# Decoding 64-bit weight words with two VectorE operations and one more ScalarE operation

## The chip, the cores and the metric

The kernel runs on one core of one Trainium2 chip. The metric is the device time of one execution in microseconds; the times below are of one core and of the same program, so they are compared directly. The core has TensorE (matrix products, "PE" in the profile, its weight loads "PEld"), VectorE ("DVE"), ScalarE ("ACT"), GpSimd ("POOL") and SyncE ("SP"), which issues most of the transfers.

## The reference

The kernel computes attention with a compressive memory for 4 sequences of 576 tokens and 8 heads of 64, and feeds the result through a two-layer expert with a sigmoid gate.

```python
scores = scale * np.matmul(q, k.transpose(0, 1, 3, 2))      # causal mask, softmax -> a
local = np.matmul(a, v)
q_p = phi(q)                                                # where(q > 0, q, exp(q) - 1) + 1
mem_out = einsum(q_p, M_prev) / (einsum(q_p, z_prev)[..., None] + 1e-06)
x = g * mem_out + (1 - g) * local                           # g = sigmoid(beta), per head
h = x @ w_in                                                # 2304 x 512 by 512 x 2048
out = (h * sigmoid(1.702 * h)) @ w_out                      # by 2048 x 512
```

The two weight matrices `w_in` and `w_out` arrive as 64-bit floats, all else as 32-bit floats. The kernel reads the 64-bit numbers as pairs of 32-bit words and makes 32-bit floats of them on the chip.

## The kernel before

**Stages.** The first 256 queries of sequence 0 are handled by themselves (`first_queries`, lines 286 to 431): scores, softmax, transposes, and the memory part, for four pairs of heads. Then 16 pairs (sequence, two heads) follow in slots, with a plan that gives each step a slot and a priority (`at`, `step`, `plan_prep`, `plan_attend`). Between their steps TensorE is filled with the first expert product (`first_moe`, line 748): chunks of 256 or 320 tokens against 16 weight blocks of 128 columns, each block 12 products per chunk (4 slices of the inner dimension, times high by high, low by high and high by low parts). Its results go to DRAM (`gd`). From about 420 us on they are read back, gated, split and multiplied by the second matrix (line 988).

**Weights.** A block of weights is 128 x 512 numbers of 64 bits, a tile `wraw` of 128 x 512 x 2 whole words: index 0 of the last dimension is the lower half of a number, index 1 the upper half. Each block goes through `load` (one transfer of 512 KB on SP's queue), `scale` (ScalarE reads the upper half as a 32-bit float and multiplies it by 2^-112, which brings the exponent into the range of 32 bits), `bits` (VectorE shifts this left by 3, puts in the sign, and puts in the top three bits of the lower half), `high` (ScalarE rounds to the matrix format) and a subtraction on GpSimd for the low part. Sixteen blocks of `w_in` go this way (`conv_unit`, line 200). `w_out` has ten blocks that `decode` (line 833) handles during the attention stage and six in `conv_pair` (line 896); both use `bit_ops` (line 826). The raw tiles of `w_in` share buffers with other tiles: blocks 0, 1, 6, 7, 12 and 13 lie in a pool of two, blocks 2, 3, 10, 11, 14 and 15 in another of two, and blocks 4 and 8 as well as 5 and 9 in buffers that first hold inputs of the first queries; the load of block 4 takes the one of `fz`, which GpSimd reads at line 151 (`fqm<-fq,fz`).

**Order.** The program is recorded with a scheduler that simulates the engines and sets the order of the instructions on each. High priority, slots and manual dependences (`add_manual_dep`, without a wait where it says NOSYNC) only bound it. In `scale` such a dependence puts each decode behind the one before (`state["behind"]`). Each engine then works through its own list in that order, SP with its transfers too.

## Time and profile before

| | |
|---|---|
| runs | 616.58, 617.18, 617.86 us; median 617.18 |
| profiled execution | 620.55 us, its span 618.8 us |
| TensorE busy | 595.2 us, 96% |
| VectorE busy | 422.5 us, 68% |
| ScalarE busy | 348.0 us, 56% |
| GpSimd busy | 214.3 us, 35% |
| granted clock of TensorE | 1.0 in all slices |

The span is the time from the first to the last instruction; what lies around it makes up the rest of the execution. The page shows the span also in 40 equal slices, with the busy share of each in tenths:

```profile
PE   6799999999999999999999999999899999999997
...
DVE  5968985666668576676565435759589668856974
ACT  5667766555456445355454333356686865676451
...
DMA  8775442443255355365342114532735832471002
```

A slice is 15.5 us long. In the first two TensorE is busy 60 and 70%, later 90% or more but for two.

### The profile page before, as it was taken

Reading aid. Unit: us, or ns where it says so; the run is one execution under the profiler, and the core shown is the slowest. Engines: PE = TensorE matmul, PEld = TensorE weight load, DVE = VectorE, ACT = ScalarE, POOL = GpSimd, SP = SyncE. Lnnn points to the kernel's source line nnn. Section 1 sums busy time; section 2 is a strip of 40 time slices with the busy share of each in tenths; the row PEclk is TensorE's granted clock in tenths of the full one; section 3 lists DMA queues with packets and bytes.
Section 4 is the critical chain, followed back from the end, with each engine's and each line's share of the span. In section 5 each row is a group of like instructions: output and inputs, shape, how many; then the busy total and the mean of one; then the engine's idle time right before and its main releaser. Section 6 shows DMA issues by size and latency. Waiting matters only on the chain.

```text
span 618.8 us, 11404 instructions
## 1 busy us (share of the span) xinstructions
PE 595.2 (96%) x4000; PEld 518.2 (84%) x4000; DVE 422.5 (68%) x1022; ACT 348.0 (56%) x811; POOL 214.3 (35%) x279
## 2 busy tenths in 40 slices
PE   6799999999999999999999999999899999999997
PEld 4466767777787888887888889999799999999997
DVE  5968985666668576676565435759589668856974
ACT  5667766555456445355454333356686865676451
POOL 4756565544536235344334221141502401320000
PEclk9999999999999999999999999999999999999999
DMA  8775442443255355365342114532735832471002
GB/s 269 256 245 155 166 135 91 131 126 101 73 174 194 94 162 176 86 195 160 95 136 64 54 59 163 172 132 75 255 117 133 268 110 54 147 249 62 26 1 76
DMA packets 46985, 84.11 MB, mean 136 GB/s; under 512 B 5328, under 2 KB 33232, under 8 KB 46928
## 3 DMA queue, kind: packets, MB, share of 16 engines
q1 hardware_dynamic: 40688, 61.36, 30.4%
q0 software_dynamic: 6240, 22.02, 11.3%
q8 instruction: 31, 0.51, 0.3%
q14 instruction: 26, 0.21, 0.1%
HBM read 59.77 MB, written 23.59 MB: 135 GB/s over the span
## 4 chain that ended last, share of the span: by engine, by line
PE 70%; DVE 9%; ACT 9%; DMA 6%; issue 4%; POOL 1%; DVEq 0%; ACTq 0%; POOLq 0%; SPq 0%
PE acc L988 28%; PE pm L129 19%; PE ps L129 8%; PE po L129 7%; PE pt L138 7%; ACT a L547 2%; DMA qr<-in_vq_dram 2%; DMA gd<-hk 2%; DVE ps L541 2%; DMA wraw<-in_w_out_dram 1%; DVE qp L496 1%; DVE wo L151 1%; DVE st L151 1%; DMA g<-gd 1%; ACT wo L143 1%
## 5 line engine op out<-in xcount | busy, mean ns | idle before, releaser
L129 PE MATMUL pm<-xh,wi 128*128 128x320 f32 (+1 forms) x1024 | 218.6, 304 | 1.7 <-POOL wi L151 1.4
L129 PEld LDWEIGHTS pm<-xh,wi 128*128 128x128 f32 x1024 | 164.8, 189 | 7.4 <-issue 3.1
L988 PE MATMUL acc<-oh,wo 128*128 128x384 f32 x672 | 158.7, 337 | 2.2 <-ACT oh L143 2.2
L129 PE MATMUL pm<-xl,wi 128*128 128x256 f32 (+1 forms) x512 | 151.7, 298 | 0.1
L988 PEld LDWEIGHTS acc<-oh,wo 128*128 128x128 f32 x672 | 120.2, 188 | 3.1 <-ACT oh L143 2.9
L550 POOL TENSOR_SCALAR a<-a,sm,g 128x512 f32<-128x512 f32 (+3 forms) x112 | 76.5, 694 | 129.6 <-DVE sm L601 98.6
L151 DVE TENSOR_TENSOR ol<-g,oh 128x768 fp32r<-128x768 f32 x84 | 82.2, 981 | 46.1 <-ACT oh L143 45.8
L988 PE MATMUL acc<-ol,wo 128*128 128x384 f32 x336 | 100.5, 338 | 0.5 <-DVE ol L151 0.4
L129 PEld LDWEIGHTS pm<-xl,wi 128*128 128x128 f32 x512 | 96.4, 189 | 0.5 <-DVE xl L151 0.3
L547 ACT ACTIVATE a<-ps,nm 128x256 f32<-128x256 f32 (+2 forms) x112 | 59.8, 540 | 65.6 <-DVE nm L541 65.6
L143 ACT ACTIVATE oh<-g 128x768 fp32r<-128x768 f32 x84 | 70.4, 842 | 44.0 <-PE acc L988 32.7
L541 DVE CUSTOM_DVE_ANT_0 ps<-ps,mask 128x256 f32<-128x256 f32 (+4 forms) x144 | 67.2, 506 | 38.8 <-PE ps L129 37.9
L129 PE MATMUL ps<-kqf 128*128 128x288 f32 (+4 forms) x288 | 71.4, 478 | 3.0 <-ACT at L547 1.4
L935 POOL DMA_DIRECT2D g<-gd x48 | 34.7, 724 | 114.3 <-DVE ol L151 66.3
L988 PEld LDWEIGHTS acc<-ol,wo 128*128 128x128 f32 x336 | 61.9, 188 | 1.8 <-DVE ol L151 1.7
L143 ACT ACTIVATE hk<-pm 128x256 f32<-128x256 f32 (+1 forms) x76 | 30.8, 408 | 44.3 <-PE pm L129 36.9
L138 PE MATMUL pt<-ident,a 128*128 128x128 f32 x296 | 53.2, 273 | 0.1
L941 ACT ACTIVATE g<-g 128x768 f32<-128x768 f32 x48 | 39.7, 839 | 15.9 <-DMA g<-gd 13.5
L129 PEld LDWEIGHTS po<-e,vr 128*64 128x64 f32 x416 | 29.9, 137 | 20.1
L151 DVE TENSOR_TENSOR g<-g,g 128x768 f32<-128x768 f32 x48 | 45.6, 951 | 0.0
L129 PE MATMUL po<-e,vr 128*64 128x320 f32 (+3 forms) x416 | 45.4, 359 | 0.0
L129 PEld LDWEIGHTS ps<-kqf 64*128 64x128 f32 (+1 forms) x288 | 30.3, 189 | 15.1 <-issue 5.3
(126 smaller groups left out, 776.6 us busy)
## 6 DMA issues: line engine op xcount, KB each, us to landing
g<-gd POOLq DMA_DIRECT2D x48, 384.0 KB, 4.7
gd<-hk SPq DMA_DIRECT2D x64, 160.0 KB, 1.9
wraw<-in_w_in_dram SPq DMA_DIRECT2D x16, 512.0 KB, 5.1
gd<-hk SPq DMA_DIRECT2D x64, 128.0 KB, 2.0
kqf<-in_kq_dram SPq DMA_DIRECT2D x12, 608.0 KB, 5.6
vr<-in_vq_dram SPq DMA_DIRECT2D x16, 320.0 KB, 4.9
wraw<-in_w_out_dram SPq DMA_DIRECT2D x10, 512.0 KB, 4.0
qr<-in_vq_dram SPq DMA_DIRECT2D x12, 320.0 KB, 3.0
```

The costliest lines, as they stand in the source:

```text
L129: x = nc.tensor.matmul(out, l, r, start=start, stop=stop)
L138: state["att"] = nc.tensor.transpose(out, in_, idn).ins.name
L143: return nc.scalar.activation(out=dst, in_=src, func=AF.Copy, **kw)
L151: return (nc.vector if eng == "V" else nc.gpsimd).tensor_tensor(out=dst, in0=a, in1=b, op=op)
L496: nc.vector.scalar_tensor_tensor(out=P["qp"][:, T0:].rearrange("p t (h d) -> p t h d", h=2), in0=qv(), scalar=0.0, in1=qm, op0=ALU.max, op ...
L541: nc.vector.tensor_tensor_reduce(out=ps, in0=ps, in1=mk, op0=ALU.add, op1=ALU.min, scale=-0.125, scalar=1e38 if j == 0 else nm[:, j - 1:j] ...
L547: return nc.scalar.activation(out=a, in_=ps, func=AF.Exp, scale=-1.0, bias=nm, accum_out=sm)
L550: return (nc.vector if eng == "V" else nc.gpsimd).tensor_scalar(out=a, in0=a, scalar1=r, scalar2=gcol, op0=ALU.mult, op1=ALU.mult)
L935: x = nc.gpsimd.dma_start(t, gd[4 * kh + p][:, :, t0:t0 + QN].rearrange("i p t -> p i t"))
L941: x = nc.scalar.activation(out=t, in_=t, func=AF.Gelu_apprx_sigmoid)
L988: nc.tensor.matmul(acc[b, j][:, :QN], W[2 * p + kk][:, WPART[i], sp, 128 * j:128 * j + 128], mv[:, kk], start=first and p + kk == 0 and sp ...
```

## The change

A new helper `low_words` is one ScalarE instruction per block: it reads the lower halves as unsigned whole numbers, multiplies by 0.936 x 2^-29, and writes the nearest whole number (0 to 7) back to the place of the lower half. `bit_ops` moves up and is now used by all three places. It shifts the scaled upper half left by 3 and puts in that number in one VectorE instruction, and puts in the sign in a second one; the shift as an instruction of its own is gone. In `conv_unit` and `conv_pair` the result goes straight to the second tile. In `conv_unit` the next block's scaling is put behind `low_words` of this block instead of behind its scaling. `low_words` itself has no dependence but on its data.

```diff
--- before.py
+++ after.py
@@ -197,6 +197,18 @@
 
     wb = {}
 
+
+    def low_words(raw):
+        return nc.scalar.activation(
+            out=raw[:, :, 0], in_=raw[:, :, 0].bitcast(mybir.dt.uint32), func=AF.Copy, scale=0.936 * 2.0 ** -29)
+
+    def bit_ops(raw, si, r):
+        x = nc.vector.scalar_tensor_tensor(
+            out=r, in0=si, scalar=3, in1=raw[:, :, 0], op0=ALU.logical_shift_left, op1=ALU.bitwise_or)
+        nc.vector.scalar_tensor_tensor(
+            out=r, in0=raw[:, :, 1], scalar=-2 ** 31, in1=r, op0=ALU.bitwise_and, op1=ALU.bitwise_or)
+        return x
+
     def conv_unit(slot, dst, src, rp, rkw, wp, wkw, sp, skw):
         box = {}
 
@@ -215,22 +227,17 @@
             for name in (state["behind"], state.get("late A")):
                 if name is not None:
                     tc.add_manual_dep(x.ins, name, NOSYNC, reason="raw words")
-            state["behind"] = x.ins.name
+            state["behind"] = low_words(box["raw"]).ins.name
 
         def bits():
             raw, si = box["raw"], box["s"].bitcast(I32)
             if "r" not in box:
                 box["r"] = sp.tile([128, DM], F32, name="wr", **skw)
-            x = nc.vector.tensor_scalar(out=si, in0=si, scalar1=3, scalar2=None, op0=ALU.logical_shift_left)
+            x = bit_ops(raw, si, box["r"].bitcast(I32))
             if "late V" in state:
                 tc.add_manual_dep(x.ins, state["late V"], NOSYNC, reason="raw words")
             for name in state.pop("bits", ()):
                 tc.add_manual_dep(x.ins, name, NOSYNC, reason="raw words")
-            nc.vector.scalar_tensor_tensor(
-                out=si, in0=raw[:, :, 1], scalar=-2 ** 31, in1=si, op0=ALU.bitwise_and, op1=ALU.bitwise_or)
-            nc.vector.scalar_tensor_tensor(
-                out=box["r"].bitcast(I32), in0=raw[:, :, 0], scalar=29, in1=si,
-                op0=ALU.logical_shift_right, op1=ALU.bitwise_or)
 
         def high():
             x = copy("A", dst[:, 0], box["r"])
@@ -823,13 +830,6 @@
     HERE = (2, 3, 5, 6, 7)
     raw2 = {}
 
-    def bit_ops(raw, si, r):
-        nc.vector.tensor_scalar(out=si, in0=si, scalar1=3, scalar2=None, op0=ALU.logical_shift_left)
-        nc.vector.scalar_tensor_tensor(
-            out=si, in0=raw[:, :, 1], scalar=-2 ** 31, in1=si, op0=ALU.bitwise_and, op1=ALU.bitwise_or)
-        nc.vector.scalar_tensor_tensor(
-            out=r, in0=raw[:, :, 0], scalar=29, in1=si, op0=ALU.logical_shift_right, op1=ALU.bitwise_or)
-
     def decode(i):
         kk, h = HERE[i // 2], i % 2
         if h == 0:
@@ -842,6 +842,7 @@
         def scale():
             x = nc.scalar.activation(out=r, in_=raw[:, :, 1].bitcast(F32), func=AF.Copy, scale=2.0 ** -112)
             tc.add_manual_dep(x.ins, state["exp"], NOSYNC, reason="not yet")
+            low_words(raw)
 
         at(state["slot"] + 4, 56, scale)
         at(state["slot"] + 4, 57, lambda: bit_ops(raw, r.bitcast(I32), r.bitcast(I32)))
@@ -905,6 +906,7 @@
             def words():
                 s = ps_w.tile([128, DM], F32, name="ws", tag="pm2")
                 nc.scalar.activation(out=s, in_=raw[:, :, 1].bitcast(F32), func=AF.Copy, scale=2.0 ** -112)
+                low_words(raw)
                 bit_ops(raw, s.bitcast(I32), raw2[kk][:, h].bitcast(I32))
 
             at(s0 + 2, 60, words)
```

Since a scheduler sets the order, the change moves instructions on all engines, above all in the first 100 us. Three places show it. In these listings line 202 is `low_words`; lines of the changed program from 225 on stand 7 to 12 lines further down than before.

The first is ScalarE's list at the exponentials of the second pair of heads of the first queries (`fa_244`); `fqm<-fq` is the pass over the first queries, `wraw_193` are the raw words of block 0. Before:

```order
L547 ACTIVATE fa_244,fsm_203<-ps_238,nm_245 128x128
L547 ACTIVATE fa_244,fsm_203<-ps_239,nm_248 128x128
L547 ACTIVATE fa_244,fsm_203<-ps_238,nm_251 128x256
L547 ACTIVATE fa_244,fsm_203<-ps_239,nm_254 128x256
L364 ACTIVATE fqm_199<-fq_186 128x16x64
```

Now, at the same place:

```order
L554 ACTIVATE fa_244,fsm_203<-ps_238,nm_245 128x128
L202 ACTIVATE wraw_193<-wraw_193 128x512
L554 ACTIVATE fa_244,fsm_203<-ps_239,nm_248 128x128
L554 ACTIVATE fa_244,fsm_203<-ps_238,nm_251 128x256
L554 ACTIVATE fa_244,fsm_203<-ps_239,nm_254 128x256
L371 ACTIVATE fqm_199<-fq_186 128x16x64
```

The word instruction of block 0 stands behind the fifth exponential of the program and ahead of the next three.

The second is ScalarE's list at the copies of the transposed first queries (`fqt`); `ws` are scaled upper halves, `ft` transposed softmax rows, `wi0` the high part of weight block 0, `wraw_578` the raw words of block 4. Before:

```order
L143 ACTIVATE ft_362<-pt_354 128x512
L143 ACTIVATE ft_362<-pt_355 128x256
L143 ACTIVATE ft_380<-pt_372 128x512
L489 ACTIVATE qmt_177<-qr_509 128x6x64
L143 ACTIVATE ft_380<-pt_373 128x256
L143 ACTIVATE ms_601<-mr_507,gt_156 128x128
L492 ACTIVATE qmt_177<-qmt_177 128x6x64
L143 ACTIVATE fqt_387<-pt_388 128x512
L213 ACTIVATE ws_447<-wraw_445 128x512
L143 ACTIVATE fqt_387<-pt_394 128x512
L143 ACTIVATE wi0_192<-wr_438 128x512
```

Now:

```order
L143 ACTIVATE ft_362<-pt_354 128x512
L143 ACTIVATE ft_362<-pt_355 128x256
L202 ACTIVATE wraw_578<-wraw_578 128x512
L225 ACTIVATE ws_447<-wraw_445 128x512
L143 ACTIVATE fqt_387<-pt_388 128x512
L225 ACTIVATE ws_458<-wraw_456 128x512
L143 ACTIVATE fqt_387<-pt_394 128x512
L143 ACTIVATE wi0_192<-wr_439 128x512
```

The fifth word instruction and one scaling stand ahead of the first copy of `fqt`; the copies `ft_380` and the work on `qmt` went behind.

The third is TensorE's list at the value products of the first queries (`po` and `pm` at line 408, now 415); `ps<-kqf` are score products of the next pair, `pt<-ident,fq` the transposes of the first queries. Before:

```order
L397 MATMUL pt<-ident,fq 128x128 x6
L129 MATMUL ps<-kqf 128x288 x2
L397 MATMUL pt<-ident,fq 128x128 x2
L129 MATMUL ps<-kqf 128x512
L408 MATMUL po<-fqt,fm 64x256 x2
L408 MATMUL po<-ft,fv 64x256 x2
L408 MATMUL po<-ft,fv 64x128 x2
L408 MATMUL pm<-fqt,fm 64x256 x2
```

Now:

```order
L404 MATMUL pt<-ident,fq 128x128 x8
L358 MATMUL pt<-ident,fa 128x128
L359 MATMUL pt<-ident,fa 128x128
L360 MATMUL pt<-ident,fa 128x128
L415 MATMUL po<-fqt,fm 64x256 x2
L415 MATMUL po<-ft,fv 64x256 x2
L415 MATMUL po<-ft,fv 64x128 x2
L415 MATMUL pm<-fqt,fm 64x256 x2
L415 MATMUL pm<-ft,fv 64x256 x2
L415 MATMUL pm<-ft,fv 64x128 x2
L129 MATMUL ps<-kqf 128x288
```

The score products of the next pair moved from ahead of the first value products to behind those of two pairs. Further down, three transposes of `qp` and the score products of 384 columns, which stood ahead of the first weight block's 12 products, now stand behind the second block's.

## Rows read from the trace of the kernel before

**Rows 1.** The page, part 1: busy us, share of the span.

```profile
PE 595.2 (96%) x4000; PEld 518.2 (84%) x4000; DVE 422.5 (68%) x1022; ACT 348.0 (56%) x811; POOL 214.3 (35%) x279
```

**Rows 2.** Stretches: length, busy us of PE, PEld, DVE, ACT, POOL; clock, DMA.

```profile
15.00:25.00 10.00, 5.46 (x20) 3.77 (x21) 9.45 (x24) 7.36 (x21) 8.31 (x13) 1.00 0.92 333
50.00:75.00 25.00, 23.96 (x174) 18.48 (x175) 22.41 (x56) 17.39 (x47) 15.51 (x16) 1.00 0.47 145
75.00:100.00 25.00, 23.33 (x160) 16.96 (x156) 20.47 (x56) 18.54 (x49) 16.38 (x17) 1.00 0.47 155
100.00:420.00 320.00, 317.40 (x2373) 267.73 (x2374) 195.33 (x609) 156.69 (x452) 118.22 (x143) 1.00 0.39 124
```

**Rows 3.** TensorE's waits, 35 to 100 us: total, times, longest.

```profile
PE ps L129 <- ACT at L547: 1.4, 3, 0.6
PE pm L129 <- POOL wi L151: 1.4, 2, 1.0
PE ps L129 <- ACT e L143: 1.1, 3, 0.4
```

**Rows 4.** The chain that ended last, 0 to 120 us: start, length, what.

```profile
13.14 0.95 ACT fqm L366
14.12 0.94 DVE fq L369
...
23.46 1.11 PE pt L397 x4
...
50.26 1.42 PE pm L129 x12
```

**Rows 5.** Tile of raw words: count, ns min/median/max, starts.

```profile
L213 ACT ACTIVATE ws<-wraw x16: 619/640/662, 19.0 to 93.3; 128x512 f32<-128x512 f32 x16
...
L843 ACT ACTIVATE r<-wraw x10: 662/682/695, 180.2 to 292.4; 128x512 f32<-128x512 f32 x10
```

**Rows 6.** Line 224, the shift of the first blocks.

```profile
L224 DVE TENSOR_SCALAR ws<-ws x16: 683/700/732, 23.3 to 94.0; 128x512 int32<-128x512 int32 x16
```

**Rows 7.** Line 827, the shift of the later blocks.

```profile
L827 DVE TENSOR_SCALAR r<-r x10: 406/456/484, 180.9 to 293.1; 128x512 int32<-128x512 int32 x10
```

**Rows 8.** Timeline, 0 to 32 us: start, length, engine, line, operation.

```profile
5.99 2.81 SPq L205 DMA_DIRECT2D wraw<-in_w_in_dram  x3
...
9.40 0.19 ACT L547 ACTIVATION_READ_ACCUMULATOR fa<-ps,nm 128x1 f32 x1
...
9.92 0.37 ACT L547 ACTIVATE fa<-ps,nm 128x128 f32<-128x128 f32 x1 [0.33 <-DVE nm L541]
...
18.89 1.41 POOL L151 TENSOR_TENSOR fqm<-fq,fz 128x256 f32<-128x256 f32 x2
...
19.56 1.29 ACT L143 ACTIVATE ft<-pt 128x256 f32<-128x256 f32 x3
...
20.32 0.33 SPq L205 DMA_DIRECT2D wraw<-in_w_in_dram  x1
```

**Rows 9.** Line 205, the load of words issued between 4 and 5 us.

```profile
L205 SPq DMA_DIRECT2D wraw<-in_w_in_dram x1: 619/619/619, 4.3 to 4.3; - x1
...
DMA to landing us min/median/max: 8.0/8.0/8.0
```

**Rows 10.** Line 205, loads of words issued about 8 us.

```profile
DMA to landing us min/median/max: 9.9/10.0/10.2
```

**Rows 11.** DMA issues at 20.3 us: size, us from issue to landing.

```profile
wraw<-in_w_in_dram SPq DMA_DIRECT2D x1, 512.0 KB, 4.5
```

**Rows 12.** Timeline, 22 to 50 us.

```profile
24.18 0.60 ACT L143 ACTIVATE fqt<-pt 128x512 f32<-128x512 f32 x1 [0.24 <-PE pt L397]
...
36.93 0.92 PE L129 MATMUL ps<-kqf 64*128 64x384 f32 x4
37.04 0.38 ACT L143 ACTIVATE xh<-po 128x256 fp32r<-128x256 f32 x1 [0.20 <-PE po L408]
...
37.77 0.50 PE L129 MATMUL pm<-xh,wi 128*128 128x256 f32 x2
```

## The prediction

> **What bounds the kernel now.** The page's busy line comes first: TensorE is busy 96% of a span of 618.8 us, with VectorE at 68% and ScalarE at 56% behind it [rows 1]. An average over stages says little, so the next view is the table by stretches [rows 2]. From 100 to 420 us the reader sees TensorE busy 317.4 of 320 us: hardly anything that another engine gains or loses there moves the end. Between 50 and 100 us it is busy 47.3 of 50, and between 15 and 25 us only 5.5 of 10, while VectorE is busy 9.45 of those 10. So the head of the program is where time can still be lost or won, and what is lost there is never made up: the later stretches have no idle time to give back. The third view is who ends TensorE's waits between 35 and 100 us: ScalarE with exponentials and copies (1.4 and 1.1 us), and GpSimd with the low half of a weight block (1.4 us in two waits) [rows 3]. VectorE is not among them. The fourth is the chain of waits in the head [rows 4]: it goes through ScalarE's second pass over the first queries at 13.14, from there to VectorE at 14.12, and on to TensorE's transposes at 23.46. ScalarE is on the path there, although its mean load is the lower one.
>
> **What the change removes and adds.** Each of 32 weight blocks (16 of the first matrix, 10 + 6 of the second) loses one VectorE instruction, gets one ScalarE instruction, and keeps two VectorE instructions of the kind that it had.
> - Removed: 16 shifts of 0.700 us in the first 96 us [rows 6], 10 of 0.456 us between 180 and 294 us [rows 7], and 6 later ones shaped like the first 16. That is 11.2 + 4.6 + 4.2 = 20.0 us of VectorE.
> - Added: a ScalarE copy with a scale over 512 strided words, in place. No row shows that form (unsigned words in, whole numbers out at a stride). The nearest are the existing copies of the other half, 0.640 us into PSUM and 0.682 into SBUF [rows 5]. The low bound is the shortest of these, 0.619; the high bound is that the strided write doubles the elements, about 0.95, as the pass over 1024 elements takes on the chain [rows 4]. I take 0.64, with 0.6 from start to start where instructions follow closely: 32 x 0.64 = 20.5 us of ScalarE. An instruction added to an engine that works in order can't cost less than nothing there.
> - The two VectorE instructions left read one plain and one strided operand, as two of the three did; I leave their time as it is.
>
> By load alone it is an exchange of equals: per block 0.700 less on VectorE, 0.64 more on ScalarE, and the latency of a block (one copy and three bit operations before, two copies and two bit operations now) stays the same within 0.1 us. The Trainium skill ("ScalarE: Activation LUTs", Rules for kernel authors) puts plain arithmetic on VectorE and not on ScalarE, which speaks against this move. The trace bears that out only for the ten blocks shifted in SBUF (0.456 against 0.682) and not for the rest (0.700 against 0.640). The same page's price (What ACT_TABLE_LOAD costs) of 186 ns + 0.833 ns an element makes 613 ns, an estimate, and 19.6 us in all in place of 20.5.
>
> **The second matrix: nothing.** Ten of its decodes lie between 180 and 294 us [rows 7] and the other six later in the same stretch, where TensorE is busy 99% with expert products that don't wait for them [rows 2]. The exchange there is hidden by TensorE's own work; without that cover it would cost 10 x (0.682 - 0.456) = 2.3 us. I take 0, bounds -0.3 to +1.
>
> **The first 45 us: this is the term.** The new instruction has no order given by hand, so the scheduler puts it where it expects the words to have landed. The order of ScalarE after the change shows the first one behind the fifth exponential of the program. ScalarE takes its instructions in order, so a load that lands later holds up all that follows.
> 1. First wait. ScalarE reaches that place at 9.40 + 0.19 = 9.59 [rows 8]. The load was issued at 4.3 and landed 8.0 us later [rows 9], at 12.3; nothing ahead of it on SP's queue moves. ScalarE stands for 2.7 us, works 0.6, and the exponential that began at 9.92 begins at about 12.95: +3.0. Queued behind are the three other exponentials of that pair and the two passes over the queries, so VectorE's step at 14.12 comes at about 17.1 and what follows on VectorE and GpSimd shifts with it. TensorE's transposes of the queries move from 23.46 to about 26.7 (+3.2).
> 2. Words two to four: their loads go between 5.99 and 8.80 [rows 8], the last landing 10.2 us or less behind its issue [rows 10], so by 19.0. ScalarE comes to the second at about 17, to the fourth at about 20.5: no wait, 3 x 0.6 = 1.8 us of work, of which I put half into waits for VectorE that it had anyway.
> 3. Second wait. The fifth word instruction now stands ahead of the two copies of the transposed queries. Its load needs the buffer that GpSimd's product at 18.89 reads: that ended at 20.30 and the load went at 20.32 [rows 8]. GpSimd's product waits for step 1, so the load goes at about 23.5 and, with 4.5 us to landing [rows 11], lands at about 28.0. ScalarE, whose copies in front ended at 19.56 + 1.29 = 20.85 [rows 8], comes there at 20.85 + 3.0 + 0.9 = 24.7, and stands for 3.3 us. With the word instruction and one decode copy behind it (0.6 each) the first copy of the queries begins at 29.2, not 24.18 [rows 12]: +5.0.
> 4. TensorE's value products need that copy. Before, three score products of the next pair stood ahead of them and were done by then; now the order shows these behind the first values, so TensorE has both kinds to do from about 29.8 on. ScalarE has three more word instructions before the last copy of the first chunk of attention outputs, but also idle time to put them into. Adding its instructions up in the new order at their present durations, that copy moves from 37.04 [rows 12] to about 42.2.
> 5. The first weight block began at 37.77 [rows 12]; 12 products take 1.42 us [rows 4], so it ended at 39.2. Now its last quarter waits for that copy (0.4), the subtraction on VectorE (0.4) and its own last products (0.2): end at about 43.2, with two scores (0.92 [rows 12]) and three transposes (0.28 each at most [rows 4], I take half) put off behind it, 1.3 us. The delay is 43.2 - 39.2 + 1.3 = 5.3 us.
>
> **What comes back.** TensorE's waits of 1.4 us for a block's low half [rows 3] can go in part, since blocks are decoded earlier in the new order; of the 2.5 us of waits for ScalarE there I count little, as ScalarE gets more to do. I take 1.3 us back. Bounds: all 5.3 (TensorE finds its idle time elsewhere), or none, with up to 8 x 0.35 = 2.8 on top if the word instructions, eight of them ahead of that copy, take 0.95 each: 0 to +8.1. The value I take is +4.0.
>
> **The sum.** 618.8 + 4.0 = 622.8 us of span; the profiled execution took 620.55 with what lies around the span, so 624.55 under the profiler. The median of the runs shown, 617.18, lies 3.37 below the profiled execution, so a run without it should take 617.18 + 4.0 = 621.2 us.
>
> **The rivals.**
> - The delay is swallowed. For it: TensorE is idle 2.7 us between 50 and 100 us and 4.5 between 15 and 25 [rows 2], and decoded blocks could fill such holes. Against it: most of TensorE's waits after 35 us are ended by ScalarE [rows 3], which gets more work. 617.2, from 616 to 618.4.
> - VectorE was the limit of the head, and its 11.2 us less there decide. For it: 9.45 of 10 us busy at 15 to 25 [rows 2] and 22.4 of 25 later. Against it: the rows on TensorE's waits name ScalarE and GpSimd [rows 3]. It decides if the words have landed when ScalarE comes to them, so that steps 1 and 3 do not occur; then the four first blocks save 4 x 0.70 on the chain before 37 us, and a little later: -2.8, 614.4 us. This is the other side.
> - ScalarE becomes the limit up to 100 us. It is busy 17.4 + 18.5 of 50 us there [rows 2]; seven or eight more word instructions make that 41 of 50, and each stands where the scheduler expects its load to land, not where it lands. Seven waits of up to 0.6 us in front of exponentials add 4: 617.2 + 8 = 625.2. That the instruction does not cost what I take (0.95, not 0.64) ends at about the same place, +6.8.
>
> **Chances.** The forecast 0.60, of its own from 618.5 to 623.5; ScalarE as the limit or the dearer instruction 0.13; swallowed 0.14; VectorE decides 0.13. About 0.2% (1.2 us) can be told from no change, so slower 0.73, within 0.14, faster 0.13. The range runs from 615.8 to 625.0: it leaves out most of the faster case and the end of the slowest.
>
> **What would show it.** Right: ScalarE's row of the first word instruction has an idle time of 2 to 3 us ended by the load of the words, the fifth one of 3 us; the first copy of the queries begins near 29, the first chunk's last copy near 42; TensorE's idle time before 45 us grows by 4 to 5 us and hardly changes after 100. Wrong in step 1 or 3 if those idle times are below 1 us. Wrong in what comes back if the head is 5 us late and the end is not, or if waits for ScalarE between 50 and 100 us grow by more than 2 us. Wrong in the price if the word instruction's mean is over 0.75 us.

## The result and the profile after

Four runs of the changed kernel took 625.79 to 627.47 us, median 626.6, against 617.52 (616.58 to 620.1) for four runs of the kernel before. The ratio is 1.014 with a 95% interval from 1.0106 to 1.0175: slower by about 9 us (6.6 to 10.8). The forecast was 621.2 us with a range up to 625.0. Its direction was right, its size was not. The kernel before took 619.5 us in the mean of 115 later runs, so the 617.18 from which the forecast started was at the low end; the differences below go by ratios to runs made side by side.

The page's busy line [rows 1] reads now:

```profile
PE 593.2 (95%) x4000; PEld 515.6 (83%) x4000; DVE 404.3 (65%) x990; ACT 366.1 (59%) x843; POOL 222.0 (36%) x279
```

VectorE lost 18.2 us, ScalarE gained 18.1 us. The table by stretches, same columns as [rows 2]:

```profile
15.00:25.00 10.00, 3.34 (x12) 1.79 (x12) 7.23 (x27) 8.85 (x28) 8.21 (x11) 0.54 0.87 308
50.00:75.00 25.00, 24.00 (x165) 18.14 (x165) 17.07 (x50) 19.56 (x51) 18.17 (x18) 1.00 0.51 164
75.00:100.00 25.00, 24.47 (x174) 18.05 (x173) 19.55 (x56) 19.97 (x51) 18.73 (x18) 1.00 0.48 161
100.00:420.00 320.00, 314.77 (x2348) 262.96 (x2347) 185.52 (x593) 166.79 (x472) 121.33 (x145) 1.00 0.39 122
```

TensorE is busy 2.1 us less between 15 and 25 us, and idle longer before 45 us was forecast. But it is also busy 2.6 us less between 100 and 420 us, where the forecast had no loss at all.

ScalarE's timeline in the head (start, length, instruction, in brackets the idle time before it and what ended it):

```profile
12.15 0.65 ACT L202 ACTIVATE wraw<-wraw 128x512 int32<-128x512 uint32 x1 [2.48 <-DMA wraw<-in_w_in_dram]
12.70 0.35 ACT L554 ACTIVATE fa<-ps,nm 128x128 f32<-128x128 f32 x1
...
26.20 0.70 ACT L202 ACTIVATE wraw<-wraw 128x512 int32<-128x512 uint32 x1 [2.35 <-DMA wraw<-in_w_in_dram]
...
28.12 0.60 ACT L143 ACTIVATE fqt<-pt 128x512 f32<-128x512 f32 x1 [0.32 <-PE pt L404]
...
40.28 0.39 ACT L143 ACTIVATE xh<-po 128x256 fp32r<-128x256 f32 x1
```

The two waits stand where the forecast put them. The exponential that began at 9.92 [rows 8] begins at 12.70, the first copy of the queries at 28.12 instead of 24.18, and the last copy of the first chunk at 40.28 instead of 37.04 [rows 12]. TensorE's timeline shows the last quarter of the first weight block waiting for that copy, and when the second expert product begins:

```profile
37.91 0.50 PE L129 MATMUL pm<-xh,wi 128*128 128x256 f32 x2
...
40.72 0.50 PE L129 MATMUL pm<-xh,wi 128*128 128x256 f32 x2 [1.84 <-ACT xh L143]
...
43.53 0.92 PE L129 MATMUL ps<-kqf 64*128 64x384 f32 x4
...
440.37 0.52 PE L990 MATMUL acc<-oh,wo 128*128 128x384 f32 x2
```

The same work (two weight blocks, three transposes, the scores of 384 columns) was done at 40.70 before and at 43.53 + 0.92 = 44.45 now: 3.75 us late. How late depends on the profile that is compared, since TensorE's clock came back at a different time in each (last section): in a later profile of the kernel before (c0 below) this work was done at 40.25, which makes it 4.2 us, and in that of e14, whose head has the work of the kernel before and where the clock came back early, at 37.75, which makes it 6.7. In the first profile of the kernel before, the second expert product begins at 434.81, and in c0 here:

```profile
434.06 0.52 PE L988 MATMUL acc<-oh,wo 128*128 128x384 f32 x2
```

So 5.6 us are lost by then against the first profile, 6.3 against c0 and 8.4 against e14 (432.00). Whichever is taken, 1.7 to 2.1 us of this are lost between 45 and 440 us.

Line 202, all word instructions, with what ended ScalarE's idle time before them:

```profile
L202 ACT ACTIVATE wraw<-wraw x32: 651/682/713, 12.1 to 408.4; 128x512 int32<-128x512 uint32 x32
...
its engine sat idle before it (us, times) until:
  DMA wraw<-in_w_out_dram: 34.4, 15
  DMA wraw<-in_w_in_dram: 8.0, 7
```

The median price is 0.682 us (0.64 was taken), and 22 of 32 stand and wait for their load. The larger sum, 34.4 us, belongs to the second matrix. Most of that is time that ScalarE had idle anyway; but some of it lies in front of exponentials that TensorE needs. The dearest place, ScalarE first, then TensorE, whose transposes wait for the exponential:

```profile
201.11 0.65 ACT L202 ACTIVATE wraw<-wraw 128x512 int32<-128x512 uint32 x1 [2.99 <-DMA wraw<-in_w_out_dram]
201.66 0.67 ACT L554 ACTIVATE a<-ps,nm 128x512 f32<-128x512 f32 x1
...
202.48 0.44 PE L138 MATMUL pt<-ident,at 128*128 128x128 f32 x2 [1.30 <-ACT a L554]
```

TensorE's waits from 100 to 420 us (total, times, longest) name the result: exponentials 3.5 us in six waits. In the profiles of the kernel before, the first of these rows is 1.0 us in three and 0.8 us in two waits, 0.5 at the longest.

```profile
PE pt L138 <- ACT a L554: 3.5, 6, 1.3
PE pt L138 <- ACT at L554: 0.8, 2, 0.5
```

The Trainium skill ("ScalarE: Activation LUTs", What ACT_TABLE_LOAD costs) gives an instruction with constant scale 186 ns and 0.833 ns an element, an estimate of 613 ns for 512 elements; this trace shows 682, some 70 ns more, and the measurement decides. The ten scalings into SBUF, which write without a stride, took 682 as well [rows 5], so the strided write in place is not what makes it dearer.

### The profile page after: what moved, and what is told of

The parts are those of the page before. It is cut to its first block, busy times and chain, and to the rows that moved or that the text cites. A ratio compares the mean times of both kernels' runs of the same rounds, so it can differ in the third digit from the quotient of the medians.

```text
span 623.9 us, 11395 instructions
## 1 busy us (share of the span) xinstructions
PE 593.2 (95%) x4000; PEld 515.6 (83%) x4000; DVE 404.3 (65%) x990; ACT 366.1 (59%) x843; POOL 222.0 (36%) x279
## 4 chain that ended last, share of the span: by engine, by line
PE 69%; DMA 10%; ACT 8%; DVE 8%; issue 3%; POOL 2%; SPq 1%; ACTq 0%; DVEq 0%; POOLq 0%
PE acc L990 25%; PE pm L129 19%; PE ps L129 8%; PE po L129 8%; PE pt L138 7%; DMA wraw<-in_w_out_dram 3%; DMA wraw<-in_w_in_dram 3%; ACT a L554 2%; DVE st L151 2%; DMA qr<-in_vq_dram 1%; DMA gd<-hk 1%; DVE wo L151 1%; ACT wraw L202 1%; DVE ps L548 1%; ACT e L143 1%
## 5 line engine op out<-in xcount | busy, mean ns | idle before, releaser
L557 POOL TENSOR_SCALAR a<-a,sm,g 128x512 f32<-128x512 f32 (+3 forms) x112 | 81.0, 734 | 127.4 <-DVE sm L608 94.0
L151 DVE TENSOR_TENSOR ol<-g,oh 128x768 fp32r<-128x768 f32 x84 | 80.8, 965 | 42.5 <-ACT oh L143 39.3
L129 PE MATMUL ps<-kqf 128*128 128x288 f32 (+4 forms) x288 | 69.2, 472 | 1.7 <-ACT at L554 1.1
L202 ACT ACTIVATE wraw<-wraw 128x512 int32<-128x512 uint32 x32 | 21.8, 680 | 42.4 <-DMA wraw<-in_w_out_dram 34.4
```

The source lines that it names most:

```text
L129: x = nc.tensor.matmul(out, l, r, start=start, stop=stop)
L151: return (nc.vector if eng == "V" else nc.gpsimd).tensor_tensor(out=dst, in0=a, in1=b, op=op)
L202: return nc.scalar.activation(out=raw[:, :, 0], in_=raw[:, :, 0].bitcast(mybir.dt.uint32), func=AF.Copy, scale=0.936 * 2.0 ** -29)
L557: return (nc.vector if eng == "V" else nc.gpsimd).tensor_scalar(out=a, in0=a, scalar1=r, scalar2=gcol, op0=ALU.mult, op1=ALU.mult)
```

## The experiments

Each was timed in several rounds beside runs of the kernel before on the same chip. The differences in us are (ratio - 1) x 619.5, the mean of 115 such runs of the kernel before; expectations written earlier took differences of medians and vary from them by a few tenths.

| kernel | ratio, 95% interval | us |
|---|---|---|
| c0 unchanged | 0.9996 (0.9974 to 1.0018) | -0.2 |
| e1 word instruction pinned, both matrices | 1.0077 (1.0047 to 1.0108) | +4.8 |
| e2 first matrix alone | 1.0095 (1.0062 to 1.0128) | +5.9 |
| e3 second matrix alone | 1.0059 (1.0032 to 1.0086) | +3.7 |
| e4 waits without work | 1.0211 (1.0171 to 1.0251) | +13.1 |
| e5 work without waits | 1.0102 (1.0065 to 1.0138) | +6.3 |
| e6 relief of VectorE alone | 0.9939 (0.9918 to 0.9960) | -3.8 |
| e7 second matrix, pinned | 1.0033 (1.0004 to 1.0062) | +2.0 |
| e8 first matrix, pinned | 1.0032 (1.0008 to 1.0056) | +2.0 |
| e9 first four blocks, pinned | 1.0004 (0.9979 to 1.0029) | +0.2 |
| e10 first seven blocks, pinned | 0.9993 (0.9965 to 1.0021) | -0.4 |
| e11 first matrix, words on GpSimd | 1.0149 (1.0107 to 1.0191) | +9.2 |
| e12 waits without work, second matrix | 1.0062 (1.0039 to 1.0086) | +3.8 |
| e13 work without waits, second matrix | 1.0045 (1.0023 to 1.0067) | +2.8 |
| e14 second matrix, ten early blocks | 1.0017 (0.9995 to 1.0040) | +1.1 |
| e15 second matrix, six late blocks | 1.0070 (1.0042 to 1.0098) | +4.3 |
| e16 relief alone, first matrix | 0.9930 (0.9908 to 0.9951) | -4.3 |
| e17 relief alone, second matrix | 0.9999 (0.9981 to 1.0017) | -0.1 |

### c0, e2, e3: which matrix

c0 is the kernel before, unchanged. e2 keeps the change in `conv_unit` and gives `decode` and `conv_pair` the three VectorE operations back; e3 does the opposite:

```diff
-            state["behind"] = low_words(box["raw"]).ins.name
+            state["behind"] = x.ins.name
...
-            x = bit_ops(raw, si, box["r"].bitcast(I32))
+            x = nc.vector.tensor_scalar(out=si, in0=si, scalar1=3, ...
```

> The kernel before, unchanged. It gives a second trace of it, because the profiled execution of before (620.55 us) lay 3.4 us above the median of its runs, while the profiled execution of the changed kernel (625.79) was the lowest of its four. All theories: 617.5 us within 0.5. If the first trace was an unusually late execution, the span here is about 615.5 to 616 us, and the difference to the changed kernel's span (623.9) is 8 us and not 5; the second trace then shows in which stretch the first one lost its 3 us.

> The change for the 16 blocks of the first matrix alone; the 16 blocks of the second are decoded with three VectorE instructions as before. Theory of the waits: the two waits of about 2.4 us in the head stay, and with them a delay of 3.8 to 4.5 us: 621 to 622.5. The 16 waits of about 2.3 us at the second matrix are gone. Theory of the load: 10.9 us of ScalarE in a head where it is on the path: about the whole difference, 624 to 626. Theory that the second matrix costs nothing (the prediction): 626, like the changed kernel.

> The change for the 16 blocks of the second matrix alone; the first matrix is decoded with three VectorE instructions as before, so the head keeps its order. Theory of the waits: the ten word instructions between 170 and 300 us stand in front of exponentials for about 2 us each, and TensorE loses some tenths of a microsecond at each: 620 to 622, with ScalarE's idle time of about 20 us or more ended by the loads of the second matrix. Theory of the load, and the prediction: TensorE covers it, 617 to 618.

Measured: -0.2, +5.9 and +3.7 us. The two halves add up to 9.6, the whole change to 9: within the noise the costs add. The second matrix, which the forecast counted at nothing, makes up two fifths.

### e1, e7, e8: the word instruction pinned

A dependence in the order only (no wait) puts each word instruction behind the scaling of its own block, so that it can't stand ahead of a load that the scaling would not have waited for.

```diff
-    def low_words(raw):
-        return nc.scalar.activation(
+    def low_words(raw, behind=None):
+        x = nc.scalar.activation(
...
+        tc.add_manual_dep(x.ins, behind.ins.name, NOSYNC, reason="words")
```

> The change as it is, but each of the 32 word instructions on ScalarE is ordered behind the scaling of the same block (order only, no wait). The work on ScalarE and VectorE is that of the changed kernel; the word instruction can no longer stand where its load has not landed. Theory of the waits (ScalarE stands in front of words that have not landed, and holds up exponentials and copies behind): 616 to 619 us, and the rows of the word instruction show no idle time ended by a load. Theory of the load (21.8 us more on ScalarE is what costs): 623 to 627, like the changed kernel. Theory of the reshuffled order (any new order costs): somewhere between, 619 to 623.

> Only the 16 blocks of the first matrix changed, with the word instruction ordered behind its block's scale. Without the ordering this was +5.7 us over before. If waits for loads are the whole cost of the first matrix, the relief of VectorE shows alone: -2 to -4 us, as where the third VectorE operation was left out (-3.8). If ScalarE's added work costs too: the difference between both matrices pinned (+4.8) and the second alone pinned (+2.0), so about +2.8, at least +1. Near 0 would mean that load and relief cancel.

> Only the 16 blocks of the second matrix changed, with the word instruction ordered behind its block's scale. Without the ordering this was +3.6 us. Waits theory: back to within 1 us of before, since the 2 to 2.5 us waits for the loads in front of the exponentials are gone. Load theory: +2 to +3.6 us, about half of the +4.8 us that both matrices pinned cost.

Measured: +4.8 with both, +2.0 with the first matrix alone, +2.0 with the second. The line table of e1 shows that the pinning did what it says, no idle time in front of 32 word instructions:

```profile
L202 ACT ACTIVATE wraw<-wraw 128x512 int32<-128x512 uint32 x32 | 21.8, 681 | 0.0
```

So the place of the instruction costs 3.9 us of 5.9 at the first matrix and, less surely, 1.7 of 3.7 at the second (the two intervals overlap). What stays is not a wait of the word instruction for its load.

### e4, e12: the wait without the work

All three VectorE operations stay; a ScalarE instruction of one element reads each raw block and is placed as the word instruction was (the edit at the first matrix; the other two places get `touch(raw)` in the same way).

```diff
+    def touch(raw):
+        return nc.scalar.activation(
+            out=one, in_=raw[:, 0:1, 0].bitcast(mybir.dt.uint32), func=AF.Copy, scale=0.936 * 2.0 ** -29)
...
-            state["behind"] = x.ins.name
+            state["behind"] = touch(box["raw"]).ins.name
```

> The kernel before with all three VectorE operations kept, and 32 tiny ScalarE instructions (128 x 1) added that only read one element of each raw block, placed by the same rule as the word instruction of the change (not ordered behind the block's scale). Waits theory (the cost is ScalarE standing at an instruction whose load has not landed, with softmax exponentials behind it): nearly the whole of what pinning gave back and more, +4 to +8 us over before. Load theory (the cost is 32 x 0.68 us more work on ScalarE): within 1 us of before.

> The kernel before with all three VectorE operations, and tiny ScalarE reads (128 x 1) of the raw words added for the 16 blocks of the second matrix only, placed by the same rule as the word instruction there. This is the wait at the second matrix without its work. Waits theory for the second matrix: +1.5 to +5 us, as much as or more than the +3.6 us that the changed decode of these blocks cost. Load theory: within 1 us of before.

Measured: +13.1 for 32 and +3.8 for the 16 of the second matrix. The line's own view in e4:

```profile
L203 ACT ACTIVATE one<-wraw x32: 185/203/226, 12.4 to 413.6; 128x1 f32<-128x1 uint32 x32
...
its engine sat idle before it (us, times) until:
  DMA wraw<-in_w_out_dram: 30.3, 14
  DMA wraw<-in_w_in_dram: 11.2, 7
```

32 x 0.203 = 6.5 us of ScalarE's time, a third of what the change adds, cost at least as much as the whole change. The wait with hardly any work is enough to make this kernel slower. It was dearer than I expected (+4 to +8), partly, it seems, because TensorE's clock fell twice more, as in the profiled execution (stretch, TensorE busy, granted clock):

```profile
48.00:55.00 7.00, 6.72 (x16) 0.51 0.09 32
55.00:89.00 34.00, 30.77 (x224) 1.00 0.55 169
89.00:93.00 4.00, 4.00 (x14) 0.57 0.10 33
```

e12 shows the mechanism at the place that was shown for the changed kernel (201.11), with an instruction of one element in front (TensorE waits for the copy `e`, which stands behind the exponential):

```profile
195.32 0.20 ACT L203 ACTIVATE one<-wraw 128x1 f32<-128x1 uint32 x1 [2.98 <-DMA wraw<-in_w_out_dram]
...
196.57 0.33 PE L138 MATMUL pt<-ident,at 128*128 128x128 f32 x1 [1.17 <-ACT e L143]
```

### e5, e13: the work without the wait

All three VectorE operations stay, and the scaling is done twice (again the edit at the first matrix).

```diff
+            y = nc.scalar.activation(
+                out=box["s"], in_=box["raw"][:, :, 1].bitcast(F32), func=AF.Copy, scale=2.0 ** -112)
-            state["behind"] = x.ins.name
+            state["behind"] = y.ins.name
```

> The kernel before with all three VectorE operations kept, and the ScalarE scale of each block done twice in succession (the second writes the same values): about 0.5 to 0.7 us more work on ScalarE per block, 32 times, with no new wait for a load. Load theory: the +4.8 us that stayed when the word instruction was pinned behind its scale comes back here, +3 to +5 us. Waits theory: within 1.5 us of before. If the order or number of the VectorE operations is what stayed, this also shows nothing.

> The kernel before with the ScalarE scale done twice for the 16 blocks of the second matrix only: the work there without a wait and without relief of VectorE. Load theory: +2 to +4 us, at the passage from 380 to 450 us, where the trace of the kernel with all 32 scales doubled shows TensorE 3.9 us idle for hidden values from VectorE. Waits theory: within 1 us.

Measured: +6.3 and +2.8. So ScalarE's work costs too, without any new wait for a load. The waits theory alone falls, and so does the load theory alone. In both traces TensorE's waits from 420 to 450 us show one place, at the passage from the first expert product to the second, which the profiles of the kernel before do not have (e5's row; e13 has the same 3.9 us):

```profile
PE acc L994 <- DVE hk L146: 3.9, 1, 3.9
```

The changed kernel does not have it either: it waits there 0.8 us for `oh` and 0.4 for `ol`. So e5 and e13 show that more work on ScalarE can cost, not that the change loses in this place. They also make each block's chain one copy longer (0.6 us), which the change does not; the two effects were not separated.

### e6, e16, e17: the relief without its price

The third VectorE operation is left out and nothing put in its place (the low three bits of the fraction are missing, of all blocks or of one matrix).

```diff
-                out=si, in0=raw[:, :, 1], scalar=-2 ** 31, in1=si, op0=ALU.bitwise_and, op1=ALU.bitwise_or)
-            nc.vector.scalar_tensor_tensor(
-                out=box["r"].bitcast(I32), in0=raw[:, :, 0], scalar=29, in1=si,
-                op0=ALU.logical_shift_right, op1=ALU.bitwise_or)
+                out=box["r"].bitcast(I32), in0=raw[:, :, 1], scalar=-2 ** 31, in1=si,
+                op0=ALU.bitwise_and, op1=ALU.bitwise_or)
```

> The kernel before without the third VectorE operation of each block and with nothing in its place on ScalarE (the low three bits of the fraction are left out, so the output differs in the last places). This is the relief that the change gives to VectorE, without its price. If VectorE limits nothing, as the forecast says: within 1 us of before. If VectorE's time in the chain from load to converted block matters: 1 to 4 us faster. If the scheduler's new order of the whole program costs something by itself: slower by 1 to 4 us.

> The third VectorE operation left out for the 16 blocks of the first matrix only (the low three bits of the fraction are missing there), nothing added on ScalarE; the second matrix as before. If VectorE's time matters in the first 100 us, as the forecast's rival said: -2 to -4 us, most of the -3.8 of both matrices together. If the -3.8 comes from the second matrix or from the new order: within 1 us.

> The same for the 16 blocks of the second matrix only. If the relief counts in the first 100 us alone: within 1 us of before. If it counts at the passage between the two expert matrices: -1.5 to -4 us.

Measured: -3.8, -4.3 and -0.1. The change does give something, all of it at the first matrix: VectorE is a limit of the head. The fair comparison is with e14 (below), whose head is that of the kernel before and whose clock came back at about the same time. Stretches of e16, columns as [rows 2]:

```profile
25.00:50.00 25.00, 22.92 (x160) 16.70 (x160) 18.88 (x55) 19.23 (x51) 15.65 (x17) 0.98 0.65 213
50.00:75.00 25.00, 23.89 (x177) 18.10 (x176) 18.57 (x53) 18.93 (x50) 16.80 (x18) 1.00 0.61 197
75.00:100.00 25.00, 23.92 (x169) 17.73 (x169) 17.50 (x51) 16.87 (x47) 14.76 (x16) 1.00 0.33 111
```

and of e14:

```profile
25.00:50.00 25.00, 23.09 (x151) 15.88 (x151) 21.36 (x61) 19.40 (x50) 15.84 (x16) 0.98 0.64 213
50.00:75.00 25.00, 23.96 (x176) 18.07 (x175) 22.14 (x57) 17.54 (x47) 15.86 (x17) 1.00 0.56 176
75.00:100.00 25.00, 23.40 (x157) 17.12 (x156) 19.72 (x55) 17.84 (x48) 14.96 (x16) 1.00 0.39 126
```

TensorE's busy times differ by 0.3 us in all, but it gets through 506 products (of several sizes) in place of 484; so here the busy time does not tell of progress. The second expert product begins 3.6 us earlier, in e16 and in e14:

```profile
428.40 0.52 PE L986 MATMUL acc<-oh,wo 128*128 128x384 f32 x2
...
432.00 0.52 PE L1001 MATMUL acc<-oh,wo 128*128 128x384 f32 x2
```

TensorE's waits for the exponentials of `at` and for `e` as in [rows 3] are gone in e16 from 35 to 100 us. What is there instead:

```profile
PE pm L129 <- POOL wi L151: 1.2, 2, 1.0
PE pm L129 <- ACT wi L143: 1.1, 1, 1.1
PE pt L138 <- ACT a L545: 1.0, 2, 0.8
```

With two smaller rows these are 4.1 us, against 4.3 in the first profile of the kernel before: the sum of the waits does not show the gain, and where on the way it arises stays open.

### e14, e15: where in the second matrix

e14 changes the ten blocks of `decode` only, e15 the six of `conv_pair`; the other place keeps three VectorE operations (here e15's edit of `decode`, against the changed kernel).

```diff
-            low_words(raw)
...
-        at(state["slot"] + 4, 57, lambda: bit_ops(raw, r.bitcast(I32), r.bitcast(I32)))
+        at(state["slot"] + 4, 57, lambda: bit_ops3(raw, r.bitcast(I32), r.bitcast(I32)))
```

> Only the ten blocks of the second matrix that are decoded early (between 180 and 294 us in the kernel before) changed, word instruction placed as in the change. If the waits of 2 to 2.5 us in front of exponentials are the cost of the second matrix: +2 to +4 us, nearly all of the +3.6. If the six later blocks near 380 to 410 us cost it: within 1 us of before.

> Only the six later blocks of the second matrix changed, word instruction placed as in the change. If ScalarE's work at the passage between the two expert matrices is the cost: +2 to +4 us. If the early ten cost it: within 1 us of before.

Measured: +1.1 (not distinct from 0) and +4.3. So most of it is at the six (the two add up to 5.4 against 3.7 for e3, within the noise), but not where I expected. In e14 all ten word instructions stand and wait for their load, 23.1 us in all, and this costs little. The scalings of the six run from some 377 us on, into a buffer whose pool opens only when the attention stage is over. The word instruction works in place and needs no such buffer, and the order lets it run as soon as the words are expected. ScalarE's timeline of e15:

```profile
281.12 0.58 ACT L566 ACTIVATE a<-ps,nm 128x384 f32<-128x384 f32 x1 [2.68 <-DVE nm L560]
...
283.08 0.68 ACT L202 ACTIVATE wraw<-wraw 128x512 int32<-128x512 uint32 x1 [1.29 <-DMA wraw<-in_w_out_dram]
283.66 0.56 ACT L566 ACTIVATE a<-ps,nm 128x384 f32<-128x384 f32 x1
...
378.73 1.20 ACT L919 ACTIVATE ws<-wraw 128x512 f32<-128x512 f32 x2 [0.49 <-DVE xl L151]
```

The first of them stands 95 us ahead of its scaling, in the attention stage, between the two exponentials of a pair of scores: the second begins 1.29 + 0.58 us later than it could. Between 270 and 295 us TensorE is busy 23.41 us there, against 24.52 in the first profile of the kernel before. That is one late place; the later ones (387.10 with 1.50 us of wait in front of the copies `wo`, 401.71 with 3.13) I could not follow to a wait of TensorE, and how the 4.3 us are shared among them stays open.

### e9, e10, e11: is there a better version

e9 and e10 keep the two VectorE operations (pinned) for the first four or seven blocks of the first matrix only, all others as before. e11 gives the word instruction of the first matrix to GpSimd.

```diff
-            x = bit_ops(raw, si, box["r"].bitcast(I32))
+            x = (bit_ops if two else bit_ops3)(raw, si, box["r"].bitcast(I32))
...
-        x = nc.scalar.activation(
-            out=raw[:, :, 0], in_=raw[:, :, 0].bitcast(mybir.dt.uint32), func=AF.Copy, scale=0.936 * 2.0 ** -29)
+        x = nc.gpsimd.tensor_scalar(
+            out=raw[:, :, 0], in0=raw[:, :, 0].bitcast(mybir.dt.uint32),
+            scalar1=0.936 * 2.0 ** -29, scalar2=None, op0=ALU.mult)
```

> Only the first four blocks of the first matrix decoded in two VectorE operations, their word instruction ordered behind the scale; the other 28 blocks as before. With both matrices pinned the first copy of hidden values came about 1.2 us earlier than in the kernel before, and the loss came between 68 and 94 us, where the later blocks are decoded. If that reading holds: 1 to 2 us faster than before. If the relief has to be on all blocks to count, or ScalarE's load counts at once: within 1 us, or slower.

> As the kernel with the first four, with the first seven blocks of the first matrix. If ScalarE's load decides only after some 60 us: 1 to 3 us faster than before. If each block's word instruction costs the same: between the kernel with four and that with sixteen, about +1.

> The 16 blocks of the first matrix decoded in two VectorE operations, with the word instruction on GpSimd in place of ScalarE (the same multiplication by a constant into whole numbers). It takes ScalarE's load and its wait out, and gives GpSimd, busy 14.7 to 16.4 of 25 us between 25 and 100 us, 16 more instructions, 0.7 to 1.2 us each as its present ones of that size. If ScalarE's load was what stayed after pinning: 1 to 4 us faster than before. If GpSimd limits in its turn (TensorE's waits for the low half of a block grow from 1.4 us): 2 to 8 us slower.

Measured: +0.2, -0.4 and +9.2. Four or seven blocks: relief and price cancel, no gain. GpSimd takes far longer for the instruction than I assumed (1.63 us), and VectorE waits for it:

```profile
L202 POOL TENSOR_SCALAR wraw<-wraw 128x512 int32<-128x512 uint32 x16 | 26.1, 1629 | 1.4
...
L210 DVE SCALAR_TENSOR_TENSOR wr<-ws,wraw 128x512 int32<-128x512 int32 x16 | 11.0, 687 | 3.9 <-POOL wraw L202 3.9
```

No version that computes the full numbers beat the kernel before.

### The account

First matrix: relief of VectorE -4.3 (e16); pinned, +2.0 (e8), so the added work and the order that comes with it cost 6.3; unpinned, +5.9 (e2), so the waits cost 3.9 more. Second matrix: relief 0 (e17); pinned +2.0 (e7), unpinned +3.7 (e3), so about 2.0 of work and 1.7 of waits. Sum -4.3 + 6.3 + 3.9 + 2.0 + 1.7 = 9.6 against 9 measured; since the parts are differences, this sum is that of e2 and e3 and no further test. The ratios behind them are each uncertain by 1.1 to 2.0 us. Measured by themselves, the waits are larger (13.1 in e4 against 3.9 + 1.7) and the work is smaller (6.3 in e5 against 6.3 + 2.0), so the parts are not fixed prices that could be carried over. Each kernel also has an order of its own on all engines, as the scheduler simulates anew; e17 (-0.1) shows that scheduling anew need not cost anything, but no experiment takes the new order out of the other parts.

## Why the prediction was wrong

**What bounds the kernel.** That the head is where time is lost, and that later stretches can't give it back, held in part: 3.75 us late at 45 us, and later still at 440, so that the stretches behind the head lose time too. "VectorE is not among them" was read from who ended TensorE's waits [rows 3] and was misleading. The full view has one VectorE row, of 0.2 us; and e16 shows that VectorE's third operation at the first matrix, with the engine 90% busy between 50 and 75 us [rows 2], was worth 4.3 us. The chain of [rows 4] had it, further down than was read: the shift that the change removes (L224) and the operation behind it.

```profile
72.95 0.69 DVE ws L224
73.67 0.69 DVE ws L229
```

**The price** of the word instruction was 0.682 us for 0.64, inside its bounds: 32 x 0.042 = 1.3 us more of ScalarE. That the two remaining VectorE operations keep their time was not quite so (VectorE lost 18.2 us, not 20.0).

**The second matrix: nothing.** This is the step that failed. Taken 0 with bounds -0.3 to +1, measured +3.7 (2.0 to 5.3). The reasoning was that TensorE, 99% busy, does not wait for the decoded blocks. No row shows TensorE waiting for them, and it is beside the point: ScalarE also serves TensorE with exponentials, and an instruction placed ahead of a load's landing holds these up, as at 201.11 in the changed kernel and in e12 almost without work (+3.8). I had written down this mechanism for the head and did not apply it to the 16 instructions behind it. Had the order of ScalarE after the change been read there too, the word instructions ahead of exponentials, one of them 95 us before its scaling in e15, would have been seen. The mechanism and the total are shown, the share of each place is not: ten of the instructions cost +1.1 by themselves (e14), six +4.3 (e15), and of these only one place was followed.

**The first 45 us.** Steps 1 to 4 came out as written, each a little smaller: first wait 2.48 us (2.7), no wait at the second to fourth, second wait 2.35 (3.3), first `fqt` copy at 28.12 (29.2), last copy of the chunk at 40.28 (42.2). Step 5's delay was 3.75 us (5.3); with the comparisons given above it is 3.75 to 6.7, so that the step was too large is not shown.

**What comes back.** Taken 1.3 us of 5.3, so +4.0; the first matrix alone measured +5.9 (3.8 to 7.9), so the interval just holds the forecast. Nothing came back: in e2's profile the same work is done at 43.28 + 0.92 = 44.20, 3.5 us later than in the first profile of the kernel before (4.0 than in c0), and the second product begins at 438.20, 3.4 us later (4.1). Against these two profiles the delay was smaller and what came back was nothing, two misses that cancel: that their sum was near 4 is luck. The 1.7 to 2.1 us that the changed kernel loses between 45 and 440 us are not in e2's profile; they came with the second matrix.

**The sum.** 617.2 + 4.0 falls short of 626.6 by 5.4 us: 3.7 from the second matrix; the 1.9 that the first took over the forecast are within the noise.

**The rivals.** "Swallowed" is refuted. "VectorE decides" was real as a term (-4.3; the forecast had -2.8) and covered by larger ones of the other sign; the condition set for it, that words have landed when ScalarE comes to them, is e8, and there the added work ate it. "ScalarE becomes the limit", 625.2, came nearest with its number, and not for its reason: TensorE's waits for ScalarE between 50 and 100 us, which it expected to grow, went from 2.1 to 1.4 us. That added work can cost is what e5 shows (+6.3), with the reservation made there.

## What to carry to other kernels

An instruction added to an engine that works in order can cost more through where a scheduler puts it than through its duration: 32 reads of one element, 0.2 us each, cost 13 us here. So give a new consumer of a load the same order constraints as its older consumer, all along the program, and read the new order at each of its places; here this gave back some 4 of the 9 us. Moving work from an engine that is 68% busy to one that is 56% busy can lose, as it did here, if the second feeds the bounding engine; measure the relief alone (leave the work out) before paying for it.

## What the runs showed of the hardware

**TensorE's clock goes with the spread of the runs.** All traces but one show the granted clock at 0.50 (1.2 of 2.4 GHz) in the head, from 12.5 to 18.4 us on, after TensorE stood idle for the first softmax; it came back between 25.8 and 32.2 us, read in stretches of half a microsecond. e14 and c0 have the same work in the same order there, and are level at the scores of 512 columns (26.51 and 26.58); the clock came back at 26.2 in the one and 31.4 in the other, and the first weight block began at 34.92 and 37.31. In the first profile of the kernel before the page shows 1.0 everywhere, yet its value products (`po<-fqt`, 533 ns in the mean) ran at the pace of c0's (532) and not of e12's (405): the records of the drop seem to be missing there, and its span has the loss. Over runs of the kernel before, 44 with a mean clock of 0.986 took 620.2 us and 23 with 0.991 or 0.992 took 617.3.

**Some kernels lose the clock again.** e1, e4 and e11 fell to 0.50 a second time at 44 to 48 us, for 7 to 10 us, behind short idle times of TensorE (in e1 1.6 us of the four from 41 to 45). e8, e9, e13, e15 and e17 did so at 44 to 49 us for 3 to 4 us, e5 and e13 again near 440 us, about their wait of 3.9 us. e9 and e17 are no slower than the kernel before for all that. Stretches of e1, TensorE busy and its clock:

```profile
28.00:44.00 16.00, 14.58 (x105) 1.00 0.81 260
44.00:55.00 11.00, 10.78 (x37) 0.53 0.30 94
```

It is 98% busy at half pace: 37 products in 11 us. The mean clock over the runs of e4 is 0.975, of e11 0.981, of e5 0.983, of e2 and e13 0.984, of e1 and e8 0.986, of after 0.986, of the kernel before 0.988. At 5.3 us for 0.01, as the kernel before has it by (620.2 - 617.3) / 0.0055, that is 7 of e4's 13 us, some 4 of e11's 9.2, 2.6 of e5's 6.3, 2 of e2's 5.9 and of e13's 2.8, and 1 to 1.5 of the 9 us of the change. This is an association over runs; no kernel here set the clock, and not all small idle times brought it down (c0 idles as much between 43 and 47 us, 1.7 of four, and keeps it).

**GpSimd** took 1.63 us for a multiplication over 512 strided words in place for which ScalarE took 0.68.
